# Causal attention with two MoE layers: half-empty transposed blocks put together by two, diagonal products with V in two row tiles

## The chip, the cores and the metric

One core of a Trainium2 chip runs the whole program in one launch. The metric is the device time in microseconds (us). The kernel before was run three times: 553.40, 554.47 and 555.22 us, median 554.47. One more execution was profiled.

## What is computed

Attention with a causal mask over 2 batches x 12 heads, 448 positions, 64 values per head, then two feed-forward layers, all in float32:

```
scores = (q @ k.T) / sqrt(64); scores = where(upper triangle, -1e9, scores)
attn   = exp(scores - max); attn = attn / (sum + 1e-9)
x = attn @ v                       # 896 tokens x 768
x = relu(x @ w_in)**2 @ w_out      # 768 -> 2048 -> 768
h = x @ w_in2; y = (h - tanh(h)) @ w_out2
```

The heads are taken by pairs: 12 pairs, numbered 0 to 11, pairs 0 to 5 of the first batch. The 448 positions are seven blocks of 64, numbered 0 to 6. Block c of the queries sees the blocks 0 to c of the keys, and of block c only the lower triangle.

## The kernel before, in words

A round of the main loop (line 549, number s) works on three pairs at once: the scores of pair s, exps and scaling of pair s - 1, transposes and products with V of pair s - 2, called a. From s = 8 on (`f`) one group of 18 products of the first MoE layer (`fill`) is put between the attention's parts. The order on each engine is the order in which the code is written; nothing is rescheduled.

*Scores* (`scores`, line 264). Per query block c one matmul per head, 64 rows deep: head 0 in the upper half of the array's rows, head 1 in the lower one. Float32 matmuls run in two passes, so the trace has two records for each. The results of the seven blocks stand in four banks of PSUM (tag `s`).

*Softmax* (`maxes`, `exps`, `small`, `sums`, `recips`, `norms`). VectorE (DVE) adds the mask, copies the scores to the tile `p` in SBUF and takes the row extremum. ScalarE (ACT) makes the exps in place, DVE scales them. In `p` every block c has a region of its own; `POFF` gives its start. Blocks with an odd number of 64-column key blocks are padded to 128 columns with zeros (line 252).

*Transposes* (`transposes`, line 335). TensorE (PE) turns `p` in pieces of 128 x 128: for the key chunk kc (128 keys) and each query block c that sees any of it. That is 7 + 5 + 3 + 1 = 16 pieces per pair (`TBLK`), four to a PSUM bank; ACT copies each bank to the tile `pt` (`tcopy`, line 342: four copies of 512 columns). In the pieces with c = 2 kc one half of the keys is padding.

*Products with V* (`pv`, line 348). For kc = 0, 1, 2 a matmul 128 rows deep over all query blocks from 2 kc on (448, 320, 192 columns), and for kc = 3 one of 64 rows and 64 columns, whose V rows are the tile `vend` (partitions 0 to 63). All of it adds up in one PSUM bank (`o`). The two heads write to the two halves of the bank's partitions, side by side.

*Output of attention* (`xhi`, line 369, on ACT; `xlo`, line 373, on DVE). The result is split into a high and a low float32r part for the MoE products. `xhi(a - 1)` stands before the copies of pair a on ACT, `xlo(a - 1)` between the softmax work of later pairs on DVE; the latter frees the bank `o` for pair a.

*MoE* (`pieces`, line 381): products of 128 rows by 448 columns, three for each pair of tiles (lines 387 to 389). Its weights are decoded and split by DVE and ACT (lines 107 to 137), in doses that a budget sets per round.

Of the kernel before, what the change touches and what calls it, by code (L numbers as in the profile page):

```python
# [8 lines left out]
F32 = mybir.dt.float32  # L9
# [10 lines left out]
B, H, S, D = 2, 12, 448, 64  # L20
DM = H * D
DFF = 2048
P = 128
# [4 lines left out]
NPAIR = B * NP  # L28
NQ = S // D
# [21 lines left out]

STEPS = (((6,), (5, 0)), ((3, 2), (4, 1)))
SOFF = {6: 0, 5: 0, 0: 384, 3: 0, 2: 256, 4: 0, 1: 320}
SI = {c: i for i, c in enumerate(c for st in STEPS for cs in st for c in cs)}
TURNED = {c for st in STEPS for c in st[1]}

SUMMED = (0,)

POFF = (0, 128, 256, 512, 768, 1152, 1536)

TBLK = [(kc, c) for kc in range(4) for c in range(2 * kc, NQ)]
TBASE = {kc: TBLK.index((kc, 2 * kc)) for kc in range(4)}


@with_exitstack
def body(ctx: ExitStack, tc: tile.TileContext, qT, kT, vL, w1, w2, w3, w4, out):
    nc = tc.nc
    sb = ctx.enter_context(tc.tile_pool(name="sb", bufs=1))  # L70
    ps = ctx.enter_context(tc.tile_pool(name="ps", bufs=1, space=PSUM))

    ident = sb.tile([P, P], F32, name="ident")
    mask = sb.tile([P, S], F32, name="mask")
# [125 lines left out]
    vs = {}  # L200
# [8 lines left out]
    def load_v(b):  # L209
        t = sb.tile([P, 3, DM], F32, tag=f"v{b}", name=f"v{b}")  # L210
        nc.sync.dma_start(out=t, in_=vL[b, : 3 * P].rearrange("(t p) d -> p t d", p=P))
        if b == 0:
            vs["end"] = slot(7, [D, B, DM], F32, "vend")
            nc.sync.dma_start(out=vs["end"], in_=vL[:, 3 * P :].rearrange("b p d -> p b d"))
        vs[b] = [t[:, 0], t[:, 1], t[:, 2], vs["end"][:, b]]

    load_qk(0)
# [11 lines left out]

    nc.gpsimd.memset(mask, 0.0)  # L230
    for j in range(2):
        r = mask[D * j : D * j + D, S - D :]
# [15 lines left out]
    prob = [slot(i, [P, 2048], F32, f"p{i}") for i in range(3)]  # L248
    for i in range(3):
        for c in range(0, NQ, 2):  # L250
            e = POFF[c] + D * (c + 1)
            nc.vector.memset(prob[i][:, e : e + D], 0.0)

    sc = {}
    stat = {}
    pt = {}
    tb = {}
    ob = {}
# [5 lines left out]
    def scores(n, t):  # L264
        q, k = qk[n]
        banks = []
        for z, cs in enumerate(step(n, t)):

            tag, bufs = ("s", 4) if n != 1 else ("t", 2) if t == 0 else ("oh"[z], 1)
            bank = ps.tile([P, 512], F32, tag=tag, bufs=bufs, name=f"s{n}_{t}_{z}")  # L270
            banks.append(bank)
            for c in cs:
                sc[n, c] = bank[:, SOFF[c] : SOFF[c] + D * (c + 1)]
        for i in range(2):
            for z, cs in enumerate(step(n, t)):
# [11 lines left out]
    def maxes(n, t, part=slice(None)):  # L287
        if n not in stat:
            stat[n] = sb.tile([P, 3, 8], F32, tag="stat", bufs=4, name=f"st{n}")
        st = stat[n]  # L290
        cs = blocks(n, t)[:: 1 if t or n == 0 else -1]
        for c in cs[part]:
            w = D * (c + 1)
            nc.vector.tensor_tensor_reduce(  # L294
                out=prob[n % 3][:, POFF[c] : POFF[c] + w],
                in0=sc.pop((n, c)),
                in1=mask[:, S - w :],
                scale=-0.125,
                scalar=3e38,
                op0=ALU.add,  # L300
                op1=ALU.min,
                accum_out=st[:, 0, SI[c] : SI[c] + 1],
            )
# [31 lines left out]
    def transposes(n, t):  # L335
        tag, bufs = ("h", 1) if t == 2 and n < NP else ("t", 2)
        bank = tb[n, t] = ps.tile([P, 512], F32, tag=tag, bufs=bufs, name=f"t{n}_{t}")
        for i, (kc, c) in enumerate(TBLK[4 * t : 4 * t + 4]):
            o = bank.rearrange("p (i j q) -> p i j q", j=2, q=D)[:, i, :: -1 if c in TURNED else 1]
            nc.tensor.transpose(o, prob[n % 3][:, POFF[c] + P * kc : POFF[c] + P * kc + P], ident)  # L340

    def tcopy(n, t):
        if t == 0:
            pt[n] = slot(3 + n % 2, [P, 16, P], F32, f"pt{n}")
        bank = tb.pop((n, t))
        nc.scalar.copy(out=pt[n][:, 4 * t : 4 * t + 4], in_=bank.rearrange("p (i q) -> p i q", q=P))  # L346

    def pv(n, kcs):
        b, hp = divmod(n, NP)
        if 0 in kcs:  # L350
            ob[n] = ps.tile([P, 512], F32, tag="o", bufs=1, name=f"o{n}")
        o = ob[n]
        for kc in kcs:
            r = P if kc < 3 else D
            m = NQ - 2 * kc
            for j in range(2):
                h = 2 * hp + j
                nc.tensor.matmul(  # L358
                    o[D * j : D * j + D, P * kc : S],
                    lhsT=vs[b][kc][:r, D * h : D * h + D],  # L360
                    rhs=pt[n][:r, TBASE[kc] : TBASE[kc] + m, D * j : D * j + D],
                    start=(kc == 0),
                    stop=(kc == 3),
                    skip_group_check=True,
                )
        if 3 in kcs:
# [182 lines left out]
    for s in range(NPAIR + 2):  # L549
        p, a = s - 1, s - 2  # L550
        ss, sp, sa = s < NPAIR, 0 <= p < NPAIR, a >= 0
        f = s - 2 >= NP
        if ss:
            budget[0] = min(budget[0], 0) + (SHARE_PAIR[f] if s > 1 else 0)
            e0, e1 = blocks(s, 0)[:: -1 if s else 1], blocks(s, 1)
        else:
            budget[0] = min(budget[0], 0) + SHARE_LAST
        if sp:
            exps(p, blocks(p, 1)[-1:])
        if ss:  # L560
# [24 lines left out]
        if ss:  # L585
            maxes(s, 0, slice(-1, None))
        if sp and s > 1:
            recips(p)
        if a >= 1:
            xlo(a - 1)  # L590
        if f and ss:
            one()
        if ss:
            exps(s, e0[:2])
        if s == 1:
            small(p)
            sums(p)
            recips(p)
        if sp:
            norms(p, (0, 1, 2) if ss else (0, 1, 2, 3, 4, 5, 6))  # L600
        if f:
            one()
        if f:
            for t in (2, 3):
                transposes(a, t)
                tcopy(a, t)
            fill(3)
        late()
        if ss:
            exps(s, e0[2:])  # L610
        relus()
        if ss:
            maxes(s, 1)
            exps(s, e1[:-1])
        if sp and ss:
# [74 lines left out]
```

## Time and profile before

| | us |
|---|---|
| median of three runs | 554.47 |
| the profiled execution | 554.28 |
| its span, first to last instruction | 552.4 |
| busy in the span: PE, DVE, ACT | 544.5, 347.6, 330.0 |
| granted clock of PE, mean | 1.00 |

The profiled execution takes 1.9 us more than its span. PE is TensorE's matmuls, PEld its weight loads, POOL is GpSimd. A matmul's duration holds the latency from its first row in to its last result out, and matmuls follow each other before the one ahead has ended, so that the durations of a group add up to more than the time it takes. What a matmul costs is read from the distance of two starts, or from differences of durations between sizes.

### The profile page before, as it was taken

The numbers are of one execution on the slowest core, as the hardware profiler recorded it, in microseconds if no ns is written. First come the engines' busy times: TensorE is split into PE (matmuls) and PEld (weight loads), VectorE is DVE, ScalarE is ACT, GpSimd is POOL, SyncE is SP. The second block draws the span as 40 slices with busy tenths as digits, with TensorE's granted clock in tenths as the row PEclk, the third lists the DMA queues.
The fourth block names the chain that finished last, engine by engine and source line by source line (L and its number), as shares of the span: only waits on it lengthen the run. The fifth ranks groups of instructions, "written<-read, shape, count | busy, mean of one in ns | idle before, by whom it ended". The sixth has DMA issues, their size and how long they took to land.

```text
span 552.4 us, 7889 instructions
## 1 busy us (share of the span) xinstructions
PE 544.5 (99%) x3038; PEld 480.9 (87%) x3038; DVE 347.6 (63%) x742; ACT 330.0 (60%) x630; POOL 1.6 (0%) x9
## 2 busy tenths in 40 slices
PE   8999999999999999999999999999999999999997
PEld 4667777899999999999999999999999999999996
DVE  5999998364534244453554688987654588887311
ACT  6999987577424266665333388776553677865100
POOL 1000000000000000000000000000000000000000
PEclk9999999999999999999999999999999999999999
DMA  8844223353443333331324130113755301016111
GB/s 259 299 149 132 109 82 97 108 171 115 135 152 115 114 115 114 115 114 58 114 66 163 58 115 1 57 58 90 237 188 171 114 1 58 0 59 217 55 50 51
DMA packets 15525, 61.85 MB, mean 112 GB/s; under 512 B 1664, under 2 KB 6400, under 8 KB 15488
## 3 DMA queue, kind: packets, MB, share of 16 engines
q1 hardware_dynamic: 15200, 61.00, 33.2%
q8 instruction: 24, 0.39, 0.3%
q10 hardware_dynamic: 288, 0.34, 0.2%
q14 instruction: 13, 0.11, 0.1%
HBM read 58.59 MB, written 2.75 MB: 111 GB/s over the span
## 4 chain that ended last, share of the span: by engine, by line
PE 93%; ACT 6%; DVE 1%; issue 0%; DVEq 0%
PE h L387 14%; PE h L389 14%; PE h L388 14%; PE o L387 14%; PE o L388 14%; PE o L389 14%; ACT p L312 3%; PE o L358 3%; PE t L340 2%; PE s L279 2%; ACT pt L346 2%; PE warm L224 1%; ACT raw L107 0%; DVE p L294 0%; ACT x L371 0%; DVE p L333 0%
## 5 line engine op out<-in xcount | busy, mean ns | idle before, releaser
L387 PE MATMUL o<-g,w 128*128 128x448 f32 x384 | 140.4, 366 | 0.0
L388 PE MATMUL o<-g,w 128*128 128x448 f32 x384 | 140.4, 366 | 0.0
L389 PE MATMUL o<-g,w 128*128 128x448 f32 x384 | 140.2, 365 | 0.0
L387 PEld LDWEIGHTS o<-g,w 128*128 128x128 f32 x384 | 72.1, 188 | 6.1
L389 PEld LDWEIGHTS o<-g,w 128*128 128x128 f32 x384 | 72.1, 188 | 6.0
L388 PEld LDWEIGHTS o<-g,w 128*128 128x128 f32 x384 | 72.1, 188 | 5.8
L387 PE MATMUL h<-x,w 128*128 128x448 f32 x192 | 72.3, 377 | 0.0
L388 PE MATMUL h<-y,w 128*128 128x448 f32 x192 | 70.6, 368 | 0.0
L389 PE MATMUL h<-y,w 128*128 128x448 f32 x192 | 70.6, 368 | 0.0
L389 PE MATMUL h<-x,w 128*128 128x448 f32 x192 | 70.6, 368 | 0.0
L387 PE MATMUL h<-y,w 128*128 128x448 f32 x192 | 70.6, 368 | 0.0
L388 PE MATMUL h<-x,w 128*128 128x448 f32 x192 | 70.5, 367 | 0.0
L124 ACT CAST w<-raw 128x768 fp32r<-128x768 f32 x56 | 50.5, 903 | 26.9 <-DVE raw L121 26.9
L121 DVE SCALAR_TENSOR_TENSOR raw<-raw 128x768 int32<-128x768 int32 x64 | 61.1, 954 | 5.4 <-ACT raw L107 5.4
L107 ACT ACTIVATE raw<-raw 128x768 f32<-128x768 f32 x64 | 59.1, 923 | 0.0
L137 DVE TENSOR_TENSOR w<-raw,w 128x768 fp32r<-128x768 f32 x32 | 30.6, 957 | 35.0 <-ACT w L124 34.8
L400 DVE TENSOR_TENSOR g<-r,g 128x448 fp32r<-128x448 f32 x32 | 20.0, 625 | 48.0 <-ACT g L397 48.0
L527 ACT COPY part<-o 128x448 f32<-128x448 f32 x24 | 12.8, 534 | 57.0 <-PE o L389 57.0
L135 DVE SCALAR_TENSOR_TENSOR w<-w,raw 128x768 fp32r<-128x768 f32 x32 | 30.6, 956 | 23.3 <-ACT w L124 23.3
L312 ACT ACTIVATE p<-p,st 128x256 f32<-128x256 f32 (+6 forms) x84 | 40.8, 516 | 4.2 <-DVE st L294 4.2
L387 PEld LDWEIGHTS h<-x,w 128*128 128x128 f32 x192 | 36.1, 188 | 4.0 <-issue 0.7
L389 PEld LDWEIGHTS h<-y,w 128*128 128x128 f32 x192 | 36.0, 188 | 3.4
(57 smaller groups left out, 718.5 us busy)
## 6 DMA issues: line engine op xcount, KB each, us to landing
raw<-w SPq DMA_DIRECT2D x64, 768.0 KB, 4.3
q<-qT SPq DMA_DIRECT2D x12, 224.0 KB, 5.3
k<-kT SPq DMA_DIRECT2D x11, 224.0 KB, 3.8
out<-part SPq DMA_DIRECT2D x11, 224.0 KB, 1.9
v<-vL SPq DMA_DIRECT2D x2, 1152.0 KB, 7.7
vend<-vL SPq DMA_DIRECT2D x1, 384.0 KB, 11.4
k<-kT ACTq DMA_DIRECT2D x1, 224.0 KB, 3.5
out<-part ACTq DMA_DIRECT2D x1, 112.0 KB, 1.7
```

The source lines that it names most:

```text
L107: nc.scalar.activation(h, h, AF.Prelu, scale=2.0**-112, alpha=2.0**32)
L121: nc.vector.scalar_tensor_tensor(out=lo, in0=hi, scalar=3, in1=lo, op0=ALU.logical_shift_left, op1=ALU.bitwise_or)
L124: act_late.append(lambda: nc.scalar.copy(out=st["w"][:, 0], in_=lo.bitcast(F32)))
L135: nc.vector.scalar_tensor_tensor(out=w[:, 1], in0=w[:, 0].bitcast(F32), scalar=-(1.0 - 2.0**-24), in1=f, op0=ALU.mult, op1=ALU.add)
L137: nc.vector.tensor_sub(out=w[:, 1], in0=f, in1=w[:, 0])
L312: nc.scalar.activation(p, p, AF.Exp, bias=st[:, 0, i : i + 1], scale=-1.0, **kw)
L358: nc.tensor.matmul(o[D * j : D * j + D, P * kc : S], lhsT=vs[b][kc][:r, D * h : D * h + D], rhs=pt[n][:r, TBASE[kc] : TBASE[kc] + m, D * j ...
L387: nc.tensor.matmul(h, lhsT=hi, rhs=xh, start=(k == 0), stop=False)
L388: nc.tensor.matmul(h, lhsT=hi, rhs=xl, start=False, stop=False)
L389: nc.tensor.matmul(h, lhsT=lo, rhs=xh, start=False, stop=(k == kk - 1))
L400: nc.vector.tensor_sub(out=dst[1], in0=v, in1=dst[0])
L527: nc.scalar.copy(out=part[m][:, b], in_=o)
```

## The change

The keys are stored in the order 6, 0, 1, 2, 3, 5, 4 (`KEYS`), and the regions of `p` are packed so that the diagonal block of 0 stands beside that of 6, and that of 2 beside that of 4. Each of these two pairs is turned by one transpose of 128 columns: one diagonal block then stands on partitions 0 to 63, the other on 64 to 127. The other 12 pieces have 128 full keys. So there are 14 pieces in place of 16, and the fourth copy has 256 columns.

The full products with V have 384, 256 and 128 columns. The diagonal blocks 0 and 2 (first half of `ENDS`, z = 0) and 6 and 4 (second half, z = 1) are products of 64 rows and 64 columns, the first half in the upper half of the array's rows, the second in the lower one, adding into the same bank. Between the two halves stands a wait: a memset of POOL on a tile `token` waits for the first half's last product, and the second half's first product waits for that memset. `vend` moves to partitions 64 to 127. The score matmul of block 4 is cut in two (64 and 256 columns), since its keys don't stand together any more. The mask is wider (704 columns), because the diagonal block is no longer always the last. The memsets of padding are gone.

In the loop the second half of pair a - 1 stands behind the scores of pair s; in the last two rounds, without scores, it stands behind the products of the pair after. The output parts of pairs 9 and 10 come later, and the banks of pairs 10 and 11 are of tag `s`.

```diff
+KPART = {c: ((0, D, D * (c + 1)),) for c in range(6)}
+KPART[4] = ((0, 6 * D, D), (D, D, 4 * D))
+KPART[6] = ((0, 0, S),)
-POFF = (0, 128, 256, 512, 768, 1152, 1536)
-TBLK = [(kc, c) for kc in range(4) for c in range(2 * kc, NQ)]
+KEYS = (6, 0, 1, 2, 3, 5, 4)
+POFF = (0, 1024, 512, 1152, 704, 1408, 64)
+DIAG = (0, 1, 2, 3, 0, 4, 0)
+TBLK = [(kc, (c,)) for kc in range(3) for c in range(2 * kc + 1, NQ)]
+ENDS = ((0, 6), (2, 4))
+TBLK += [(None, cs) for cs in ENDS]
...
-                        nc.tensor.matmul(sc[n, c][e : e + D], lhsT=q[r, D * c : D * c + D], rhs=k[r, : D * (c + 1)], start=(c == cs[0]), stop=(c == cs[-1]), skip_group_check=True)
+                        for o, a, w in KPART[c]:
+                            nc.tensor.matmul(sc[n, c][e : e + D, o : o + w], lhsT=q[r, D * c : D * c + D], rhs=k[r, a : a + w], start=(c == cs[0] and o == 0), stop=(c == cs[-1]), skip_group_check=True)
...
+        e = min(4 * t + 4, NT)
+        nc.scalar.copy(out=pt[n][:, 4 * t : e], in_=bank.rearrange("p (i q) -> p i q", q=P)[:, : e - 4 * t])
...
+    def pv(n):
+        tag, bufs = ("o", 1) if n < NPAIR - 2 else ("s", 4)
+        ob[n] = ps.tile([P, 512], F32, tag=tag, bufs=bufs, name=f"o{n}")
+        for kc, i in enumerate(TBASE):
+            m = NQ - 2 * kc - 1
             for j in range(2):
+                product(n, j, slice(S - D * m, S), kc, slice(0, P), pt[n][:, i : i + m, D * j : D * j + D], start=(kc == 0), stop=False)
+        pv_ends(n, 0)
+    def pv_ends(n, z):
+        for i, cs in enumerate(ENDS):
+            c = cs[z]
+            for j in range(2):
+                r, e = slice(D * z, D * z + D), D * (j ^ (c in TURNED))
+                ins = product(n, j, slice(D * c, D * c + D), c // 2, r, pt[n][r, NT - 2 + i, e : e + D], start=False, stop=(z == 1 and i == 1))
+                if z == 1 and i == j == 0:
+                    tc.add_manual_dep(ins, passed.pop(n), WAITS, reason="row tiles of one bank")
+        if z == 0:
+            p = nc.gpsimd.memset(token, 0.0).ins
+            tc.add_manual_dep(p, ins.name, WAITS, reason="row tiles of one bank")
+            passed[n] = p.name
...
             scores(s, 0)
             scores(s, 1)
+            if a >= 1:
+                pv_ends(a - 1, 1)
...
-        if a >= 1:
+        if a >= 1 and ss:
             xhi(a - 1)
+        if a == NPAIR - 1:
+            xhi(a - 2)
...
         if sa:
-            pv(a, range(4))
+            pv(a)
+            if not ss:
+                pv_ends(a - 1, 1)
...
+    pv_ends(NPAIR - 1, 1)
+    xhi(NPAIR - 2)
+    xlo(NPAIR - 2)
     xhi(NPAIR - 1)
     xlo(NPAIR - 1)
```

Between pair 1's products and pair 2's transposes PE's order was this (o1, pt1: bank and transposed tile of pair 1; s4: scores of pair 4; x2 at the end: both heads; 128x2x64: a piece whose heads are swapped):

```order
L358 MATMUL o1_375<-pt1_332,v0_108 64x192 [waits Activation_49]
L358 MATMUL o1_375<-pt1_332,v0_108 64x192
L358 MATMUL o1_375<-pt1_332,vend_110 64x64 x2
L279 MATMUL s4_0_0_387<-k4_185,q4_184 64x448 [waits DMAHW4_49,DMAHW3_49]
...
L279 MATMUL s4_1_1_396<-k4_185,q4_184 64x128 x2
L340 MATMUL t2_0_413<-ident_63,p2_116 128x2x64 [waits PE_49]
```

With the change it is this:

```order
L369 MATMUL o1_375<-pt1_334,v0_108 64x128 x2
L369 MATMUL o1_375<-pt1_334,v0_108 64x64 [waits Activation_49]
L369 MATMUL o1_375<-pt1_334,v0_108 64x64 x3
L289 MATMUL s4_0_0_390<-k4_178,q4_177 64x448 [waits DMAHW4_49,DMAHW3_49]
...
L289 MATMUL s4_1_1_399<-k4_178,q4_177 64x128 x2
L369 MATMUL o1_375<-pt1_334,vend_110 64x64 [waits Pool_49]
L369 MATMUL o1_375<-pt1_334,vend_110 64x64
L369 MATMUL o1_375<-pt1_334,v0_108 64x64 x2
L357 MATMUL t2_0_422<-ident_63,p2_116 128x2x64 [waits PE_49]
```

Two small products of the first half follow at once, and behind the scores, before the next transposes, stand the four of the second half with the wait on POOL.

At the end of the attention part, where no scores are left, PE's order is now this (h6: the first product of the MoE layer behind it):

```order
L369 MATMUL o11_1381<-pt11_1337,v1_481 64x64 [waits Activation_49]
L369 MATMUL o11_1381<-pt11_1337,v1_481 64x64 x3
L369 MATMUL o10_1308<-pt10_1255,vend_110 64x64 [waits Pool_49]
L369 MATMUL o10_1308<-pt10_1255,vend_110 64x64
L369 MATMUL o10_1308<-pt10_1255,v1_481 64x64 x2
L369 MATMUL o11_1381<-pt11_1337,vend_110 64x64 [waits Pool_49]
L369 MATMUL o11_1381<-pt11_1337,vend_110 64x64
L369 MATMUL o11_1381<-pt11_1337,v1_481 64x64 x2
L417 MATMUL h6_0_1412<-x0_66,w6_1306 128x448 [waits DVE_49]
```

Before, two products of 64 rows stood here between the 128-row ones and h6. Now pair 11's second half stands right behind its first half and pair 10's second half.

## Rows read from the trace of the kernel before

**Rows 1.** The page: busy us of the engines, share of the span, instructions.
```profile
PE 544.5 (99%) x3038; PEld 480.9 (87%) x3038; DVE 347.6 (63%) x742; ACT 330.0 (60%) x630; POOL 1.6 (0%) x9
```

**Rows 2.** Windows: stretch, length; busy us of PE, PEld, DVE, ACT, POOL; PE's clock; DMA.
```profile
38.20:49.10 10.90, 9.91 (x110) 6.76 (x109) 10.90 (x47) 10.90 (x35) 0.00 (x0) 1.00 0.43 154
58.30:67.50 9.20, 9.20 (x81) 7.20 (x79) 8.86 (x32) 8.16 (x24) 0.00 (x0) 1.00 0.26 88
```

**Rows 3.** Chain that ended last, merged: start us, us on the chain, engine and line.
```profile
28.27 3.34 ACT p L312 x13
59.16 0.87 PE t L340 x8
```

**Rows 4.** Timeline of DVE: start us, us, instruction, idle time before and its releaser.
```profile
20.26 0.17 DVE L322 TENSOR_SCALAR st<-st 128x7 f32<-128x7 f32 x1 [0.39 <-ACT p L312]
38.15 0.17 DVE L322 TENSOR_SCALAR st<-st 128x7 f32<-128x7 f32 x1 [0.86 <-ACT p L312]
67.19 0.62 DVE L400 TENSOR_TENSOR g<-r,g 128x448 fp32r<-128x448 f32 x1 [0.30 <-ACT g L397]
```

**Rows 5.** Groups by line and shape, whole span: count, busy us, mean ns of one.
```profile
L312 ACT ACTIVATE p<-p,st 128x448 f32<-128x448 f32 x12 | 8.2, 684 | 0.0
L312 ACT ACTIVATE p<-p,st 128x64 f32<-128x64 f32 x12 | 4.3, 369 | 0.0
L358 PE MATMUL o<-pt,v 128*64 128x320 f32 x48 | 8.6, 432 | 0.0
L358 PE MATMUL o<-pt,v 128*64 128x192 f32 x48 | 6.0, 326 | 0.0
```

**Rows 6.** Timeline of PE around pair 6's products with V: start us, us, instructions.
```profile
54.22 0.36 PE L388 MATMUL h<-x,w 128*128 128x448 f32 x1
54.42 0.37 PE L389 MATMUL h<-x,w 128*128 128x448 f32 x1
54.72 1.84 PE L358 MATMUL o<-pt,v 128*64 128x448 f32 x12
56.49 0.27 PE L358 MATMUL o<-pt,vend 64*64 64x64 f32 x2
...
58.27 0.47 PE L387 MATMUL h<-x,w 128*128 128x448 f32 x1
```

**Rows 7.** Timeline of PE, pair 5: the 64-row product with V and the scores after.
```profile
47.30 0.27 PE L358 MATMUL o<-pt,vend 64*64 64x64 f32 x2
47.32 0.59 PE L279 MATMUL s<-k,q 64*64 64x448 f32 x2
47.41 0.23 PE L358 MATMUL o<-pt,vend 64*64 64x64 f32 x2
47.46 0.54 PE L279 MATMUL s<-k,q 64*64 64x448 f32 x2
```

**Rows 8.** Timelines and POOL's groups: what one engine's end releases on another.
```profile
86.61 0.51 ACT L371 CAST x<-o 128x448 fp32r<-128x448 f32 x1
87.02 0.58 ACT L346 COPY pt<-t 128x512 f32<-128x512 f32 x1
87.65 0.33 PE L340 MATMUL t<-ident,p 128*128 128x128 f32 x1 [0.34 <-ACT pt L346]
100.01 0.33 PE L358 MATMUL o<-pt,vend 64*64 64x64 f32 x4
100.27 0.47 PE L387 MATMUL h<-x,w 128*128 128x448 f32 x1
L230 POOL MEMSET mask<- 128x448 f32 x1 | 0.5, 471 | 0.3 <-POOLq L683 0.3
L683 POOL MEMSET const-bfloat16-1.0<- 128x1 bf16 x1 | 0.1, 102 | 0.0
```

**Rows 9.** Timelines of PE and ACT, pair 3: the first four transposes and their copy.
```profile
31.34 0.49 PE L340 MATMUL t<-ident,p 128*128 128x128 f32 x3
31.92 0.58 ACT L346 COPY pt<-t 128x512 f32<-128x512 f32 x1
```

More of the change, by code (lines that the diff above doesn't have):

```diff
@@ L59 @@
 SUMMED = (0,)
-POFF = (0, 128, 256, 512, 768, 1152, 1536)
-TBLK = [(kc, c) for kc in range(4) for c in range(2 * kc, NQ)]
-TBASE = {kc: TBLK.index((kc, 2 * kc)) for kc in range(4)}
+KEYS = (6, 0, 1, 2, 3, 5, 4)
+POFF = (0, 1024, 512, 1152, 704, 1408, 64)
+DIAG = (0, 1, 2, 3, 0, 4, 0)
+BEFORE = D * max(DIAG)
+TBLK = [(kc, (c,)) for kc in range(3) for c in range(2 * kc + 1, NQ)]
+TBASE = [TBLK.index((kc, (2 * kc + 1,))) for kc in range(3)]
+ENDS = ((0, 6), (2, 4))
+FRONT = {c for _, c in ENDS}
+TBLK += [(None, cs) for cs in ENDS]
+NT = len(TBLK)
 @with_exitstack
@@ L73, in body @@
     ident = sb.tile([P, P], F32, name="ident")
-    mask = sb.tile([P, S], F32, name="mask")
+    mask = sb.tile([P, BEFORE + S], F32, name="mask")
     abias = sb.tile([P, 1], F32, name="abias")
@@ L212, in load_v @@
         if b == 0:
-            vs["end"] = slot(7, [D, B, DM], F32, "vend")
-            nc.sync.dma_start(out=vs["end"], in_=vL[:, 3 * P :].rearrange("b p d -> p b d"))
+            vs["end"] = slot(7, [P, B, DM], F32, "vend")
+            nc.sync.dma_start(out=vs["end"][D:], in_=vL[:, 3 * P :].rearrange("b p d -> p b d"))
         vs[b] = [t[:, 0], t[:, 1], t[:, 2], vs["end"][:, b]]
@@ L231, in body @@
     for j in range(2):
-        r = mask[D * j : D * j + D, S - D :]
+        r = mask[D * j : D * j + D, BEFORE : BEFORE + D]
         nc.gpsimd.affine_select(out=r, in_=r, compare_op=ALU.is_ge, fill=-8e9, base=0, pattern=[[-1, D]], channel_multiplier=1)
@@ L246, in hbank @@
         return ps.tile([P, 512], F32, tag=tag, bufs=bufs, name=name)[:, :S]
[L248 to L252, printed above, removed]
+    prob = [slot(i, [P, NQ * (NQ + 1) // 2 * D], F32, f"p{i}") for i in range(3)]
     sc = {}
@@ L296, in maxes @@
                 in0=sc.pop((n, c)),
-                in1=mask[:, S - w :],
+                in1=mask[:, BEFORE - D * DIAG[c] :][:, :w],
                 scale=-0.125,
@@ L337, in transposes @@
         bank = tb[n, t] = ps.tile([P, 512], F32, tag=tag, bufs=bufs, name=f"t{n}_{t}")
-        for i, (kc, c) in enumerate(TBLK[4 * t : 4 * t + 4]):
-            o = bank.rearrange("p (i j q) -> p i j q", j=2, q=D)[:, i, :: -1 if c in TURNED else 1]
-            nc.tensor.transpose(o, prob[n % 3][:, POFF[c] + P * kc : POFF[c] + P * kc + P], ident)
+        for i, (kc, cs) in enumerate(TBLK[4 * t : 4 * t + 4]):
+            o = bank.rearrange("p (i j q) -> p i j q", j=2, q=D)[:, i]
+            c = cs[0]
+            if kc is None:
+                src = prob[n % 3][:, POFF[c] + D * c :][:, :P]
+            else:
+                g = POFF[c] + P * kc + (D if c in FRONT else 0)
+                src = prob[n % 3][:, g : g + P]
+                o = o[:, :: -1 if c in TURNED else 1]
+            nc.tensor.transpose(o, src, ident)
@@ L342, in tcopy, with product @@
     def tcopy(n, t):
         if t == 0:
-            pt[n] = slot(3 + n % 2, [P, 16, P], F32, f"pt{n}")
+            pt[n] = slot(3 + n % 2, [P, NT, P], F32, f"pt{n}")
         bank = tb.pop((n, t))
-        nc.scalar.copy(out=pt[n][:, 4 * t : 4 * t + 4], in_=bank.rearrange("p (i q) -> p i q", q=P))
-    def pv(n, kcs):
+        e = min(4 * t + 4, NT)
+        nc.scalar.copy(out=pt[n][:, 4 * t : e], in_=bank.rearrange("p (i q) -> p i q", q=P)[:, : e - 4 * t])
+    def product(n, j, o, kc, rows, rhs, **flags):
@@ L349, in pv @@
         b, hp = divmod(n, NP)
[L350 to L355, printed above, removed]
-            for j in range(2):
[L357 to L365, printed above, removed]
@@ L366, in pv @@
-        if 3 in kcs:
+        h = 2 * hp + j
+        return nc.tensor.matmul(ob[n][D * j : D * j + D, o], lhsT=vs[b][kc][rows, D * h : D * h + D], rhs=rhs, skip_group_check=True, **flags).ins
+    def pv(n):
[3 more added lines that the diff above has]
+            m = NQ - 2 * kc - 1
+            for j in range(2):
+                product(n, j, slice(S - D * m, S), kc, slice(0, P), pt[n][:, i : i + m, D * j : D * j + D], start=(kc == 0), stop=False)
+        pv_ends(n, 0)
@@ new lines, in body @@
+    passed = {}
+    token = sb.tile([P, 1], F32, name="token")
+    def pv_ends(n, z):
[10 more added lines that the diff above has]
+            passed[n] = p.name
+        if z == 1:
@@ L588, in body @@
             recips(p)
-        if a >= 1:
+        if a >= 1 and ss:
             xlo(a - 1)
+        if a == NPAIR - 1:
+            xlo(a - 2)
         if f and ss:
@@ L672, in pairs, with values @@
         return np.ascontiguousarray(t.reshape(B, NP, 2, S, D).transpose(0, 1, 2, 4, 3)).reshape(B, NP, P, S)
+    def values(t):
+        t = np.ascontiguousarray(t.transpose(0, 2, 1, 3)).reshape(B, NQ, D, DM)
+        return np.ascontiguousarray(t[:, [0, 1, 2, 3, 5, 4, 6]]).reshape(B, S, DM)
     arrays = {
         "qT": pairs(inputs["q"]),
-        "kT": pairs(inputs["k"]),
-        "vL": np.ascontiguousarray(inputs["v"].transpose(0, 2, 1, 3)).reshape(B, S, DM),
+        "kT": pairs(np.concatenate([inputs["k"][:, :, D * c : D * c + D] for c in KEYS], 2)),
+        "vL": values(inputs["v"]),
         "w1": w_in(inputs["moe_w_in"]),
```

1 line of the change is left out of this document (added).

## The prediction

> **What bounds the kernel now.** I read the page first, then a table of windows, then the chain of waits, then single stretches. The page shows TensorE (PE) busy 544.5 us, 99% of the span [rows 1], but busy is not the same as bound, so the table decides. From 38.2 to 49.1 us VectorE (DVE) and ScalarE (ACT) are full and PE is not (9.91 of 10.90); from 58.3 to 67.5 PE is full and DVE has a little left (8.86 of 9.20) [rows 2]. The granted clock is 1.00 in both, the 2.4 GHz level, and nothing here idles PE long enough to expect another. So the attention part has two stretches: up to about 48 us the pairs of heads are paced by ACT and DVE, from there on by PE. After 100.3 us come only products of the two MoE layers, in which the change touches nothing; whatever is won before is kept.
>
> The chain shows the same: at 28 us 13 exps of ACT in a row, at 59 us eight transposes of PE [rows 3]. In the first stretch DVE idles only twice, 0.39 and 0.86 us, both times for ACT [rows 4]. It has 1.25 us to give, so no saving on PE or ACT can win more there.
>
> **The change part by part.** *Transposes.* 14 instead of 16 per pair. Eight take 0.87 us on the chain [rows 3], 0.109 each: **-0.22 us of PE per pair**. The fourth copy out of PSUM has 256 columns instead of 512. ACT's exps fall from 684 ns at 448 columns to 369 at 64 [rows 5], 0.82 ns per column, so it saves 0.21 us per pair on ACT.
>
> *Full products with V.* 384, 256 and 128 columns instead of 448, 320 and 192: 64 fewer in each of three, in two passes each, the two heads side by side. Matmul times include a latency, so only differences count: 432 - 326 ns for 128 columns [rows 5], 0.83 ns per column. 3 x 2 x 64 x 0.83 = **-0.32 us per pair**.
>
> *Diagonal products.* Before: one block of 64 rows, two passes, in the upper row tile. Now: two blocks there (four passes), and behind the scores two more in the lower row tile (four passes). Both kinds of array shape occur before in the same order, and each change of shape costs about 0.09 us (two h matmuls stand 0.20 apart, from h to V 0.30 [rows 6]); their number stays. What happens in the 64-row shape is seen at 47.30: the V product starts in the upper tile, 0.02 us later head 1's scores start in the lower one, its second pass comes at 47.41, and head 0's scores start at 47.46 [rows 7]. So the row tiles run side by side. In pair 6 the stretch from that product to MoE is 1.78 us (56.49 to 58.27 [rows 6]), 1.69 less the change of shape, set by the upper tile. There two passes are added: 0.11. The lower tile starts 0.14 earlier but shows two weight loads of some 0.05 uncovered, so I estimate its end 0.06 earlier, at 1.63; four passes of 0.055 and the split of score block 4 (64 + 256 columns, no more columns, 0.02) give 1.87. The later one counts: **+0.17 us per pair**. Bounds for an added pass: 0.05 (47.41 to 47.46) and 0.11 (47.30 to 47.41) [rows 7]. I take the lower, because the higher stands where the shape has just changed and no weights could be loaded ahead. That makes +0.11 to +0.5 per pair.
>
> Here the Trainium skill speaks against the change: its page "TensorEngine Tiling (Array Packing)", section "Instruction Overhead", gives every matmul about 60 cycles of overhead and advises against tiling by a size that is already small. By that, an estimate from the page, 0.025 us would go on top of each of six small passes a pair, and the sum would come out at 552.4. The 0.05 us for a pass of 64 columns shows no such addition [rows 7].
>
> *The new wait.* The first product of the second half waits for a POOL memset that waits for the first half. It stands in PE's queue, and behind it all of PE: the transposes, ACT's copies, the next pair. No row shows PE-POOL-PE. Lower bound: the last pass's own time 0.22 (two of them 0.23 [rows 7]), 0.09 from PE to another engine (the fourth transpose ends at 31.34 + 0.49 = 31.83, ACT starts at 31.92 [rows 9]), 0.10 for a 128x1 memset, 0.05 back (ACT's copy ends at 87.60, PE starts at 87.65 [rows 8]): 0.46 us. Upper bound: POOL's longest row, 0.47, with the longest idle time of its group before it, 0.30, in place of 0.10: 1.13 us [rows 8]. I take 0.46, as the work is the 128x1 row's. The cover is head 1's scores: from the start of the first half's last pass (0.11 + 2 x 0.055 = 0.22 after its first) to 1.63, so 1.41 us. Cost 0 in pairs 0 to 8; behind pairs 9 and 10 the next pair's transposes and products come between. Without scores behind it stands **pair 11** only: 0.22 + 0.46 + four passes (0.27) + 0.09 = 1.04 instead of 0.26 (from 100.01 to 100.27 [rows 8]), **+0.79**, up to 1.45.
>
> *xhi and o.* The output bank is complete about 1.9 us later, behind the scores, so ACT's cast waits there now with copies and exps behind it. It costs nothing as long as the transposes come still later: at 31.92 ACT's copy follows the fourth transpose by those 0.09, so it waits for PE already, and the cast (0.41 before its copy) has its data about then. DVE's subtraction (xlo) frees the bank for the next V, in DVE's order as before. Pair 9's cast and subtraction move a round later: the cast out of the way of the copies at 87.02 (86.61 to 87.02 is 0.41 [rows 8]); the subtraction takes the place that pair 10's had. The twelve memsets gone from DVE's start and the wider mask on POOL lie before the first scores are read; cost 0.
>
> **The sum**, against the profiled execution's own 554.28 us (0.2 under the median of the three, 554.47):
> - First stretch: ACT saves 0.21 in each of the pairs 0 to 3 before DVE's idle time at 38.15, 0.84 in all. But its copies wait for PE too, whose margin at 31.9 is 0.09 + 0.15 that PE itself gains between V and the transposes (0.32 - 0.17), on top of 0.21 from the first idle time [rows 4]; so about 0.45, and 0.21 of the last copy: **-0.7** (bounds 0 and -1.25).
> - Pair 5, from V to the scores' end, first under PE: -0.32 + 0.17 = **-0.15**.
> - Pairs 6, 7, 8: 3 x (-0.22 - 0.32 + 0.17) = **-1.1**.
> - Pairs 9 and 10, no scores behind V, both tiles side by side: 2 x (-0.22 - 0.32 + 0.11) = **-0.86**.
> - The stop of PE before 87.65 (0.34 of idle time [rows 8]) ends 0.41 earlier, while PE comes 0.21 earlier from pair 9: **-0.2**.
> - Pair 11: -0.22 - 0.32 + 0.79 = **+0.25**.
>
> Together -2.8 us: **551.5 us**. All bounds at their good end give 550.7, all at their bad one 554.6.
>
> **The rivals.**
> (a) *DVE keeps the pace.* It is full from 38.2 to 49.1 [rows 2] and idles 0.30 at 67.19 [rows 4], less than the 0.37 of a pair. Then the first stretch wins nothing, pair 5 neither, and a pair in the second 0.30: -2.8 + 0.7 + 0.15 + 0.2, 552.5 us. Against it: both idle times of the first stretch are for ACT.
> (b) *Small passes cost double*, 0.11 each as after a change of shape. Six passes at 0.055 above my price: +0.33 in pairs 5 to 8, four (+0.2) in pairs 9 to 11: -2.8 + 1.9, 553.4 us. For it: the pass at 47.30; against it: the one at 47.41. By the page named above, of the Trainium skill, it would be half of that.
> (c) *POOL answers late: slower.* If PE-POOL-PE takes R, each of the pairs 0 to 8 loses R - 1.41, and pair 11 R - 0.46. 10 R = 2.8 + 9 x 1.41 + 0.46 gives the point from which the change loses: R = 1.6 us. At 2.0 us it is 9 x 0.59 + 1.54 - 2.8 = +4.1, 558.4 us. Against it: the rows allow 1.13 at most; for it: POOL has no work after the first microseconds, so nothing shows how it wakes.
> That the change does not do what it says is excluded by the order: 14 transposes, and the wait on Pool, stand there.
>
> **How the numbers follow.** About 0.3%, 1.7 us, is what a measurement of this kernel can tell from no change. My forecast (550.5 to 552.7) 0.52, (a) 0.18, (b) 0.18, (c) 0.08, the rest 0.04. Faster by over 1.7 us, so under 552.8: nearly all of the forecast, some 0.6 of (a), a little of (b): 0.62. Same: the rest of those: 0.28. Slower: (c) and strays: 0.10. The range takes in the forecast, (a) and most of (b), with the spread of the runs before below: 550.2 to 554.0.
>
> **What would show it.** Steps right: V's first 64-row product comes 1.45 us after V's start instead of 1.77 (54.72 to 56.49), and MoE 1.95 after that instead of 1.78 (to 58.27 [rows 6]); DVE's idle time at 38 us is nearly gone; before 100 us PE stops once for POOL, about 0.5 us. Wrong: PE idle before the second half's products in every pair (c), 64-column passes 0.11 apart throughout (b), the first stretch's pairs at 5.5 to 5.7 us as before with DVE free of idle time (a).

## The result and the profile after

The changed kernel takes **548.40 us** (median of four, 548.29 to 548.79) against 554.17 for the kernel before in the same series: a ratio of 0.9898, with a 95% interval of 0.9883 to 0.9912. That is 5.8 us less, where 2.8 were forecast; the range began at 550.2, so the time lies below it. The sign was right, the size was not.

The page of the changed kernel: its busy line (it answers to [rows 1]), the granted clock and a group of MoE products:

```profile
span 546.6 us, 8248 instructions
PE 538.0 (98%) x3206; PEld 483.6 (88%) x3206; DVE 345.8 (63%) x730; ACT 327.9 (60%) x630; POOL 4.2 (1%) x21
PEclk9999999999999999999999999999999999999999
...
L417 PE MATMUL h<-y,w 128*128 128x448 f32 x192 | 69.7, 363 | 0.0
```

PE's timeline of the changed kernel (start us, us, engine, line, operation, count, idle time before and its releaser), where attention ends and at the last MoE product:

```profile
98.37 0.33 PE L369 MATMUL o<-pt,vend 64*64 64x64 f32 x4 [0.26 <-POOL token L393]
98.53 0.28 PE L369 MATMUL o<-pt,v 64*64 64x64 f32 x4
98.75 0.48 PE L417 MATMUL h<-x,w 128*128 128x448 f32 x1
...
542.89 0.37 PE L419 MATMUL o<-g,w 128*128 128x448 f32 x1
```

The same timeline of the kernel before, its last product:

```profile
548.71 0.36 PE L389 MATMUL o<-g,w 128*128 128x448 f32 x1
```

Attention ends at 98.75 instead of 100.27 [rows 8]: 1.52 us earlier. From there to the last product it is 444.14 us instead of 448.44: **4.30 us come from the two MoE layers, whose instructions are the same in both kernels.** Each layer runs in two halves, and each half has two stages: products into h, then products into o. Here is layer one's second half, first in the kernel before, then in the changed one: the first and the last product of its h stage, and of its o stage.

```profile
195.89 0.36 PE L387 MATMUL h<-x,w 128*128 128x448 f32 x1
...
254.82 0.37 PE L389 MATMUL h<-x,w 128*128 128x448 f32 x1
255.02 0.36 PE L387 MATMUL o<-g,w 128*128 128x448 f32 x1
...
313.37 0.36 PE L389 MATMUL o<-g,w 128*128 128x448 f32 x1
```

```profile
193.75 0.36 PE L417 MATMUL h<-x,w 128*128 128x448 f32 x1
...
251.16 0.36 PE L419 MATMUL h<-x,w 128*128 128x448 f32 x1
251.37 0.36 PE L417 MATMUL o<-g,w 128*128 128x448 f32 x1
...
310.00 0.37 PE L419 MATMUL o<-g,w 128*128 128x448 f32 x1
```

A stage has 288 products, so 287 distances. The h stage falls from 58.93 to 57.41 us, 205.3 to 200.0 ns a product; the o stage rises from 58.35 to 58.63, 203.3 to 204.3 ns. PE is not idle in either and the granted clock is the same. What did change for these products is where their operands stand in a partition of SBUF: the wider mask, the smaller tiles `p` and `pt` and the 4-byte token (32 after rounding) push the tiles behind them. The operands are these: the weights are in the ring of tiles w, the moving operand (the one that streams through the array) of an h product is a tile x (y in the second layer, in the same place), that of an o product one of eight tiles, the g slots. The traces hold no addresses; those in this text follow from the order and the sizes in which a kernel creates its tiles.

### The profile page after: what moved, and what is told of

It reads as the page before. It is cut to its first block, busy times and chain, and to the rows that moved or that the text cites. A ratio compares the mean times of both kernels' runs of the same rounds, so it can differ in the third digit from the quotient of the medians.

```text
span 546.6 us, 8248 instructions
## 1 busy us (share of the span) xinstructions
PE 538.0 (98%) x3206; PEld 483.6 (88%) x3206; DVE 345.8 (63%) x730; ACT 327.9 (60%) x630; POOL 4.2 (1%) x21
## 4 chain that ended last, share of the span: by engine, by line
PE 92%; ACT 4%; DVE 3%; issue 0%; DVEq 0%; POOLq 0%; ACTq 0%
PE o L419 14%; PE o L418 14%; PE o L417 14%; PE h L417 14%; PE h L419 14%; PE h L418 14%; PE o L369 3%; ACT p L322 2%; PE t L357 2%; PE s L289 2%; DVE p L304 1%; DVE p L343 1%; ACT pt L364 1%; PE warm L238 1%; ACT raw L121 0%; DVE x L405 0%
## 5 line engine op out<-in xcount | busy, mean ns | idle before, releaser
L417 PE MATMUL h<-x,w 128*128 128x448 f32 x192 | 71.5, 372 | 0.0
L417 PE MATMUL h<-y,w 128*128 128x448 f32 x192 | 69.7, 363 | 0.0
L419 PE MATMUL h<-y,w 128*128 128x448 f32 x192 | 69.6, 362 | 0.0
L419 PE MATMUL h<-x,w 128*128 128x448 f32 x192 | 69.5, 362 | 0.0
L418 PE MATMUL h<-x,w 128*128 128x448 f32 x192 | 69.4, 362 | 0.0
L418 PE MATMUL h<-y,w 128*128 128x448 f32 x192 | 69.1, 360 | 0.0
```

What stands on the lines that cost most here:

```text
L417: nc.tensor.matmul(h, lhsT=hi, rhs=xh, start=(k == 0), stop=False)
L418: nc.tensor.matmul(h, lhsT=hi, rhs=xl, start=False, stop=False)
L419: nc.tensor.matmul(h, lhsT=lo, rhs=xh, start=False, stop=(k == kk - 1))
```

## The experiments: what moved the MoE layers

Three theories: A, the place of the weights against the moving operand; B, the sizes of the big tiles; C, not addresses but the other stream of instructions. The first four runs change addresses alone.

**e1: the kernel before with a tile that nothing uses.**

```diff
+    pad = sb.tile([P, 1], F32, name="pad")
+    nc.gpsimd.memset(pad, 0.0)
     sc = {}
```

> The kernel before, with one tile more: 4 bytes in every partition, which the allocator rounds up to 32, created where the change creates its token, and cleared once by POOL. Everything created after it, the ring of weights w and four of the eight g slots among it, stands 32 bytes further (w at 32 instead of 0 modulo 64 bytes); no instruction of PE, ACT or DVE changes. Theory A (the place of the weights in SBUF against the moving operand sets the pace of the MoE products): the four stages of h products take 57.4 us instead of 58.9 each, the four of o products 0.3 more, as in the changed kernel: 549.4 us instead of 554.2, and down to 548.5 if the h products in the attention part gain as well. Theory B (it was the 1,024 bytes by which mask, probability and transposed tiles moved the others) and theory C (not addresses, but the other stream of instructions): 554.2 us, h stages 58.9.

549.56 us, ratio 0.992 (0.9906 to 0.9935). Thirty-two bytes give 4.5 us. PE's timeline, the same h stage and the end of attention:

```profile
99.97 0.47 PE L389 MATMUL h<-x,w 128*128 128x448 f32 x1
...
194.93 0.36 PE L389 MATMUL h<-x,w 128*128 128x448 f32 x1
...
252.34 0.36 PE L391 MATMUL h<-x,w 128*128 128x448 f32 x1
```

57.41 us, as in the changed kernel, from the token's 32 bytes alone and without a new stream of PE's instructions. Theory A stands; B and C fall.

**e2, e3, e4: the changed kernel with a token of 64 bytes; with everything from x on 32 bytes further; with both.**

```diff
-    token = sb.tile([P, 1], F32, name="token")
+    token = sb.tile([P, 16], F32, name="token")
...
-    abias = sb.tile([P, 1], F32, name="abias")
+    abias = sb.tile([P, 9], F32, name="abias")[:, :1]
```

> The changed kernel with a token tile of 64 bytes instead of 4 (32 after rounding): what is created after it stands 32 bytes further, w at 0 modulo 64 again. Theory A: the h stages are back at 58.9 us, o stages at 58.35, so the MoE layers lose 4.8 us: 553.2 us, and up to 554.0 if h products in the attention part lose too. Theories B and C: 548.4 us as in the changed kernel.

> The changed kernel with everything from the x tiles on 32 bytes further: x at 0 instead of 32 modulo 64 and w at 0 instead of 32, so that their distance is that of the changed kernel. If the distance between moving operand and weights counts (A1), h stages stay at 57.4 us and the time at 548.4. If the place of the weights alone counts (A2), h stages are back at 58.9: about 553.2 us. Theories B and C: 548.4.

> The changed kernel with x 32 bytes further (0 modulo 64) and everything behind the token 64 bytes further (w at 32 modulo 64 as in the changed kernel; all eight g slots at 32 as well). If the distance between x and w counts (A1), h stages are slow at 58.9 us, and o stages, where g and w now agree, fast at about 57.4: 548.4 + 6.0 - 5.0, about 549 us. If the place of the weights alone counts (A2): 548.4 us, h stages 57.4, o stages 58.6. Theories B and C: 548.4 us.

552.23 us (0.997, 0.9958 to 0.9981), 547.77 (0.9894, 0.9877 to 0.991) and 551.05 (0.9949, 0.9934 to 0.9964). e2 loses 3.8 of the 5.8 us again. e3, with both places moved and their distance kept, loses nothing: the distance counts, not the place (A1). e4's h stages are slow as A1 says; its total lies 2 us above the 549 worked out, as h is slower than in the kernel before (206.6 ns) and o less fast than hoped (202.0).

**e5, e6: all agreeing modulo 64 bytes,** the changed kernel and the kernel before.

```diff
-    nc.scalar.activation(sb.tile([P, 1], F32, name="warmexp"), abias, AF.Exp)
+    nc.scalar.activation(sb.tile([P, 9], F32, name="warmexp")[:, :1], abias, AF.Exp)
```

(e5 has e2's token as well.)

> The changed kernel with two small tiles rounded up to 64 bytes instead of 32 (warmexp and the token), so that x, all eight g slots and the w ring stand at 32 modulo 64 bytes; no instruction changes. If the distance between moving operand and weights modulo 64 bytes counts, h stages stay at 57.4 us and o stages fall from 58.6 to 58.0 as in the two runs whose g slots all agreed with w: 548.4 - 4 x 0.65 = 545.8 us. If agreement in one place costs as much in another: 548.4 or more.

> The kernel before with one small tile (warmexp) rounded up to 64 bytes instead of 32, so that x, g and w all stand at 32 modulo 64; no instruction changes. By the distance: h stages 57.4 instead of 58.9, o stages 58.0 to 58.35, attention 0.3 less: 554.0 - 4 x 1.5 - (0 to 1.4) - 0.3 = 546.3 to 547.7 us, which is less than the changed kernel as handed over. Against it the run above then gives what the change itself is worth when addresses are equal: by the attention stretch of the earlier runs -1.2 to -1.3 us; by the forecast -2.8.

548.47 us (0.9898, 0.9883 to 0.9913) and 548.71 (0.9907, 0.9891 to 0.9922): both misses. In e5 o gained (201.9 ns), but h went to 202.7; in e6 h came to 200.0, but o stayed at 203.5. Modulo 64 was too coarse. Sorted by the weights' address less the moving operand's modulo 128 the stages fell into four classes, and e9 to e11 were set up for the fastest one, 64.

**e9, e10, e11: difference 64 modulo 128** in the changed kernel, the kernel before, and e8 (below), by wider small tiles and unused pads ahead of the w ring and of two g slots.

```diff
+        if u == 0:
+            sb.tile([P, 16], F32, name="pad0")
...
+            if (l, half, m, b) == (0, 0, 0, 0):
+                sb.tile([P, 16], F32, name="pad1")
```

> The changed kernel, no instruction changed, with x and all eight g slots at 32 modulo 128 bytes and the w ring at 96, by wider small tiles and two pads of 64 bytes. The rule read from the runs so far: the spacing of two MoE products follows the weights' address less the moving operand's, modulo 128 bytes: 200.0 ns at 64, about 202.7 at 0, 205.3 at 32, 206.6 at 96. By it h stages and o stages all take 57.4 us: 548.4 - 4 x 1.2 = 543.6 us. If the rule holds for h alone and something else sets the o stages: 545.8 to 548.4 us.

> The kernel before, no instruction changed, with its addresses arranged as in the run above. By the rule all eight stages take 57.4 us: 554.0 - 4 x 1.5 - 4 x 0.95 - 0.3 = 543.9 to 544.8 us, the upper end from 549.6 (w moved by 32 bytes alone) less 4 x 1.2. The run above should then be faster than this one by what the change's instructions are worth, 1.2 us by the attention stretch; by the forecast's steps it would be 2.8.

> The changed kernel with the second half of the diagonal products between the two steps of scores and with the addresses of the first run of this group. The two gains add: 547.8 - 4.8 = 543.0 us, about 0.6 below the first run of this group. If the gain of the middle place came from elsewhere, as much as the first run.

545.13 us (0.9835, 0.9821 to 0.9848), 548.22 (0.9888, 0.9874 to 0.9901), 544.95 (0.983, 0.9816 to 0.9843): faster, yet 1.5 to 4 us short of the rule. e10's h stages took 202.2 ns at the same 64 modulo 128 at which e1's took 200.0. Modulo 256 the two differ, 64 and 192. With that every stage of every run so far stands in one table (distance of two products in ns, from the first and last start of a stage in the traces; where g slots fall into two classes both are given):

```
kernel             h: diff  ns      o: diff of the g slots       ns
before             160      205.3   128 (4 slots), 0 (4)         203.3
after, e1, e3      192      200.0   160 (4), 0 (4)               204.3
e2, e4             224      206.6   192 (4), 0 (4)               202.0
e5                 0        202.7   192 (4), 0 (4)               201.9
e6                 192      200.0   128 (4), 0 (4)               203.5
e9, e11            192      200.0   64 (6), 192 (2)              201.9
e10                64       202.2   192 (6), 64 (2)              201.1
e14, e15, e16      192      200.0   192 (8)                      200.0
```

Within the changed kernel's o stages the products of the slots at 160 stand 205.3 to 205.9 ns apart, those at 0 201.6 to 204.2. So in a mixed stage the slots at one difference don't all have one pace. Two stages don't fit: the shorter first h stage took 204.4 in e2 and 200.0 in e4, where later ones took 206.6. What else plays a part there stays open. Differences of 32 and 96 were not run. The wider mask and the smaller `p` and `pt` move others by multiples of 1,024 bytes, which is nothing modulo 256: of the change's moves only the token's 32 bytes count in this table, as e1 shows.

**e14, e15, e16: every difference at 192 modulo 256,** with the pads of e9 resized (0.6 KB a partition in all; e15 has one pad more).

> The changed kernel, no instruction changed, with every g slot and x at 160 modulo 256 bytes and the weights at 96, so that the weights' address less the moving operand's is 192 modulo 256 everywhere. Rule D256, from the runs so far (spacing of two products by that difference: 200.0 ns at 192, 202.2 at 64, 202.7 at 0, about 203.4 at 128, 205.3 to 205.9 at 160, 206.6 at 224): all eight stages take 57.4 us, 545.1 - 4 x 0.53 = 543.0 us. If o stages have a pace of their own: 545.1, as with six of the eight slots at 64.

> The kernel before, no instruction changed, with every difference at 192 modulo 256 bytes. D256: all stages at 57.4 us; 548.2 - 4 x 0.64 (h, 58.05 to 57.4) - 4 x 0.32 (o, 57.73 to 57.4) - 0.15 in the attention part = 544.2 us, so that the changed kernel at 192 is 1.2 us faster than this one. If the change is worth 2.8 at equal pace, as forecast: 545.8.

> The changed kernel with the second half of the diagonal products between the two steps of scores, every difference at 192 modulo 256. D256: 544.95 - 4 x 0.53 = 542.8 us, the fastest of all.

**543.03 us** (0.9797, 0.9784 to 0.9811), **544.54** (0.9825, 0.9811 to 0.9838) and **542.63** (0.979, 0.9777 to 0.9803): all three within 0.4 of what was written down. e14's timeline, an h stage and the o stage behind it, 57.40 us each:

```profile
98.59 0.47 PE L419 MATMUL h<-x,w 128*128 128x448 f32 x1
...
192.31 0.36 PE L419 MATMUL h<-x,w 128*128 128x448 f32 x1
...
249.71 0.36 PE L421 MATMUL h<-x,w 128*128 128x448 f32 x1
249.91 0.36 PE L419 MATMUL o<-g,w 128*128 128x448 f32 x1
...
307.31 0.36 PE L421 MATMUL o<-g,w 128*128 128x448 f32 x1
```

So at equal pace the change's own instructions are worth 544.54 - 543.03 = 1.5 us, about half of the forecast (e1 and the changed kernel, whose differences agree too, give 549.56 - 548.40 = 1.2), and the kernel before with pads beats the changed kernel as handed over by 3.9 us. By its median e16 is the fastest kernel of the study.

## The experiments: the attention part

e1 is the fair partner here: its differences are those of the changed kernel, in h and in o. Pair 7's round in e1, then in the changed kernel:

```profile
63.88 0.60 PE L360 MATMUL o<-pt,v 128*64 128x448 f32 x2
...
65.64 0.27 PE L360 MATMUL o<-pt,vend 64*64 64x64 f32 x2
65.66 0.59 PE L281 MATMUL s<-k,q 64*64 64x448 f32 x2
65.75 0.23 PE L360 MATMUL o<-pt,vend 64*64 64x64 f32 x2
65.81 0.54 PE L281 MATMUL s<-k,q 64*64 64x448 f32 x2
...
67.43 0.48 PE L389 MATMUL h<-x,w 128*128 128x448 f32 x1
...
73.00 0.59 PE L360 MATMUL o<-pt,v 128*64 128x448 f32 x1
```

```profile
63.36 0.54 PE L369 MATMUL o<-pt,v 128*64 128x384 f32 x2
...
64.80 0.38 PE L369 MATMUL o<-pt,v 64*64 64x64 f32 x5
64.97 0.59 PE L289 MATMUL s<-k,q 64*64 64x448 f32 x1
...
65.03 0.23 PE L369 MATMUL o<-pt,v 64*64 64x64 f32 x2
65.08 0.54 PE L289 MATMUL s<-k,q 64*64 64x448 f32 x2
...
66.68 0.27 PE L369 MATMUL o<-pt,v 64*64 64x64 f32 x1
66.73 0.22 PE L369 MATMUL o<-pt,vend 64*64 64x64 f32 x1
66.79 0.28 PE L369 MATMUL o<-pt,v 64*64 64x64 f32 x3
67.00 0.48 PE L417 MATMUL h<-x,w 128*128 128x448 f32 x1
...
72.36 0.54 PE L369 MATMUL o<-pt,v 128*64 128x384 f32 x2
```

From MoE to the next V 5.36 instead of 5.57 us: two transposes less, -0.21 as forecast. From V to the first 64-row product 1.44 instead of 1.76: -0.32 as forecast. From there to MoE 2.20 instead of 1.79: **+0.41, forecast +0.17**. So a round gains 0.12 instead of 0.37. The added passes hold up the scores of *both* row tiles. In the lower tile, whose scores start while the first half still fills the upper one, the first scores come 0.17 behind the first 64-row product (64.97) instead of 0.02 (65.66). In the upper tile they come 0.28 behind it (65.08) instead of 0.17 (65.81), behind the first half's last passes.

**e7: without the split of score block 4.**

```diff
-KPART[4] = ((0, 6 * D, D), (D, D, 4 * D))
+KPART[4] = ((0, D, 5 * D),)
```

> The changed kernel without the split of score block 4: its scores come from one product of 320 columns instead of 64 and 256 (keys 0 to 3 and 5 in place of 0 to 4, so the scores of one block are other ones). If the split is what makes the scores end 0.18 us later than before (measured from the first product of 64 rows), that stretch from 64-row product to MoE falls from 2.19 to 2.0 us in pairs 5 to 8: 547.7 us. If it is the first half's added passes that hold up the scores of both row tiles, the stretch falls by 0.06 at most: 548.2 us.

547.54 us (0.9881, 0.9864 to 0.9897). Pair 7:

```profile
62.96 0.54 PE L369 MATMUL o<-pt,v 128*64 128x384 f32 x2
...
66.48 0.48 PE L417 MATMUL h<-x,w 128*128 128x448 f32 x1
```

3.52 us from V to MoE instead of 3.64: the split costs 0.12 a pair, not 0.02. From V of pair 5 to V of pair 9 it is 35.54 us (45.19 to 80.73) instead of 36.02, the same 0.12 in each of four pairs. That is half of the excess of 0.24; the expectation had put all of it or 0.06 on it.

**e8: the second half between the two steps of scores** (`pv_ends(a - 1, 1)` moved up one line).

> The changed kernel with the second half of the diagonal products behind the first step of the next pair's scores instead of behind both, in pairs 0 to 9. Theory L (in the first stretch the output bank is complete too late: PE stops 0.44 us twice before V for DVE's subtraction, ACT waits 0.1 to 0.2 for the bank): these stops are gone and the first MoE product at 49 us comes 0.3 to 0.5 earlier, 548.0 us. Theory D (DVE's own work paces that stretch, the stops of PE are only what is left over): the time is 548.4, with the same 0.7 us of idle time of DVE at 38 us. If POOL's answer is needed before it is there (it is ready some 0.5 to 0.7 us after the last pass of the first half, and the first step of scores covers about 0.85), PE stops before the second half in pairs 5 to 8 and the time is 549 us or more.

547.84 us (0.9886, 0.9871 to 0.9901). The total is that of theory L, the place is not: from V of pair 1 to V of pair 5 it takes 23.73 us (20.88 to 44.61, with a stop of PE as before, now for ScalarE's copy), as in the changed kernel, 23.69 (21.66 to 45.35). A gain shows in the second stretch, 53.02 us from V of pair 5 to MoE (44.61 to 97.63) instead of 53.40, where the small passes now run between score passes. V of pair 0 comes earlier as well, at 14.54 instead of 15.30, but that is no work of this edit: in e3, with the changed kernel's instructions, it comes at 14.69. POOL's answer is there in time all the same.

```profile
44.61 0.55 PE L369 MATMUL o<-pt,v 128*64 128x384 f32 x2 [0.51 <-ACT pt L364]
```

**e12 and e13: less of DVE, less of ScalarE in the first stretch.**

```diff
+            if c == 6 and n < 5:
+                continue
```

```diff
-            w = D * (c + 1)
+            w = D if c == 6 and n < 6 else D * (c + 1)
```

> The changed kernel without VectorE's scaling of the largest score block (448 columns, 0.44 us) in pairs 0 to 4, so five operations of DVE less before V of pair 5. Theory D (DVE's own work paces the first stretch): V of pair 5 comes up to 2.2 us earlier, at 43.2 to 44.5 instead of 45.35, and the time falls by as much. Theory S (ScalarE's exps and copies pace it, DVE only waits in other places): V of pair 5 comes less than 0.5 us earlier and DVE's idle time grows by the rest.

> The changed kernel with ScalarE's exp of the largest score block cut to its first 64 columns in pairs 0 to 5 (the other columns stay without exp): 0.3 us less of ScalarE in each, six before V of pair 5. Theory S (ScalarE paces the first stretch): V of pair 5 comes 1.2 to 1.8 us earlier against V of pair 0, 28.3 to 28.9 us behind it instead of 30.05. Theory R (no engine alone: ScalarE, DVE and PE wait for each other in a ring, as taking 0.12 a pair from PE won 0.13 in all and 0.44 a pair from DVE 0.4): about 0.4 us earlier, and the idle time shows up on ScalarE.

547.73 and 547.53 us, one run each. The timelines at V of pairs 0 and 5, e12 and e13, and behind them from 14 to 50 us DVE's waits in e12 and ScalarE's in e13 (us in total, times, longest):

```profile
15.10 0.54 PE L371 MATMUL o<-pt,v 128*64 128x384 f32 x2
...
44.75 0.54 PE L371 MATMUL o<-pt,v 128*64 128x384 f32 x2 [0.45 <-DVE x L407]
...
DVE st L332 <- ACT p L322: 2.1, 3, 1.1
```

```profile
14.64 0.54 PE L369 MATMUL o<-pt,v 128*64 128x384 f32 x2
...
44.61 0.54 PE L369 MATMUL o<-pt,v 128*64 128x384 f32 x2 [0.45 <-DVE x L405]
...
ACT pt L364 <- PE t L357: 1.0, 2, 0.8
ACT x L401 <- PE o L369: 0.7, 1, 0.7
```

From V of pair 0 to V of pair 5 it takes 29.65 and 29.97 us, against 30.05 in the changed kernel (15.30 to 45.35). Runs with the changed kernel's instructions differ there: 29.88 in e14, 30.20 in e9. So of the four scalings left out on the way (1.8 us) some 0.4 came back (0.2 to 0.55 by the run that it is set against), and of the four shortened exps (1.2 us) nothing that is clear of this spread. Counted from V of pair 1 e13 seems to gain more, 23.00 against 23.69; but there V of pair 1 had come later, 6.97 us behind V of pair 0 instead of 6.36, and e9, with V of pair 1 late in the same way (6.87), shows 23.33 with nothing left out. Neither D nor S holds. With less of DVE, DVE's waits for ScalarE grow from 1.0 to 2.1 us; with less of ScalarE, ScalarE's waits for PE grow from 0.2 to 1.7. That fits theory R, the ring, but it is one run each, and what share each engine has stays open.

## Why the prediction was wrong

**The step that failed:** "After 100.3 us come only products of the two MoE layers, in which the change touches nothing; whatever is won before is kept." The instructions are untouched; their operands' addresses are not, and with them went 4.3 of the 5.8 us. The MoE products inside the attention part gained as well: it ends at 99.97 in e1 instead of 100.27. The forecast had this term at nothing. The profile of before shows the pace of 205.3 ns but not that it could be another one; the diff shows that tiles move, and I did not follow them through the allocation. The other step that failed is the price of the diagonal products beside scores (below): the change's own instructions won 1.2 to 1.5 us, not 2.8. The two errors have opposite signs: at the forecast's price for the instructions the time would lie lower still.

The attention part by the sum's own steps, the changed kernel against e1 (starts of V, us; the last row ends at MoE; V of pair 0 starts at 15.29 in e1 and 15.30 in the other):

```
                          e1              after           gain   forecast
up to V of pair 5         45.62           45.35           -0.27  -0.7
V(5) to V(6)              45.62 to 54.75  45.35 to 54.35  -0.13  -0.37
V(6) to V(9)              54.75 to 82.13  54.35 to 81.37  -0.36  -1.11
V(9) to V(11)             82.13 to 97.94  81.37 to 96.19  -0.99  -1.06
V(11) to MoE              97.94 to 99.97  96.19 to 98.75  +0.53  +0.47
```

- *Transposes, full products with V, pairs 9 and 10, pair 11*: right. PE stops for POOL once, 0.26 us in the row at 98.37, and in pair 7 the memset starts 0.35 us behind the first half's last passes (65.03 to 65.38):

```profile
65.38 0.23 POOL L393 MEMSET token<- 128x1 f32 x1 [8.83 <-PE o L369]
```

  Behind scores PE never waits for it. Rival (c) is out.
- *Diagonal products beside scores*: mis-sized, +0.41 a round instead of +0.17 (rows above). The failing sentence is that the lower row tile's end comes 0.06 earlier. It counts on that tile's scores starting 0.02 behind the first 64-row product, as before; they start 0.17 behind it, so the tile begins 0.15 later. And splitting a score block costs 0.12 (e7), not 0.02. With these two sizes the prediction's own sum for the lower tile is 1.63 + 0.15 + 4 x 0.055 + 0.12 = 2.12 us, 2.21 with the change of shape; 2.20 were measured. That PE hands out its products in the order of the program, so that a pass that waits for its tile holds up those for the other, would explain the 0.15; no run tests it. In pairs 5 to 8 all this took 1 us of the forecast, though not beyond the bound of +0.5.
- *Rival (b)*, every small pass 0.11 apart, is out: at 66.68, 66.73 and 66.79 they start 0.05 to 0.06 apart. The overhead of about 60 cycles that the Trainium skill, "TensorEngine Tiling (Array Packing)", section "Instruction Overhead", gives every matmul is not seen there as an addition to each pass; that section's own example, that a matmul of one column takes as long as one of 60, makes it a least time rather, which 64 columns can't show. The small tiles cost more than forecast all the same, by the two sizes above.
- *First stretch*: -0.27, less than the -0.7 of the sum and nearer to rival (a), whose sign, DVE without idle time, is not there. "It costs nothing as long as the transposes come still later", said of the late output bank, leaves out a wait. Waits of PE and DVE from 14 to 50 us in the changed kernel, then DVE's in e1 (us in total, times, longest):

```profile
PE t L357 <- ACT pt L364: 1.3, 2, 0.7
PE o L369 <- DVE x L405: 0.9, 2, 0.4
...
DVE st L332 <- ACT p L322: 1.0, 2, 0.7
```

```profile
DVE st L324 <- ACT p L314: 1.2, 2, 0.9
```

  PE stops twice for DVE's subtraction to free the bank, which it doesn't in e1, and DVE's idle time falls by 0.2 of 1.25 only [rows 4]. By e8 this wait is not the cause of the small gain: there PE stops for ScalarE instead, and V of pair 5 comes no earlier behind V of pair 0 (30.07 us, 14.54 to 44.61, against 30.05). What keeps the gain small stays open; e12 and e13 fit engines that wait for each other in turn.

## What to carry to other kernels

Before a change is credited with its time, compare a stage that it does not touch; if that stage moved, look at the addresses. A change that resizes or adds an SBUF tile moves every tile behind it, so measure it against the old kernel with a pad that gives the old operands the new places; here 32 bytes counted, and moves by 1,024 did not. In a kernel of back-to-back products, choose the places of weights and moving operands on purpose: here 0.6 KB of padding a partition won 9.6 us in the kernel before and 5.4 in the changed one, where the change's instructions won 1.5.

## What the runs showed of the hardware

Back-to-back products of 128x128 weights with 448 columns in four bytes started 200.0 to 206.6 ns apart at the granted clock of 1.00 (the 2.4 GHz level), by the weights' address less the moving operand's modulo 256 bytes: 200.0 at 192, 202.2 at 64, 202.7 at 0, 205.3 at 160, 206.6 at 224; between 203 and 204 where half the slots stood at 128. Two places moved together by 32 bytes changed nothing (e3). These are the paces of whole stages with one difference; one short stage at 224 took 200.0 (e4), so the difference is not the whole rule.

An obvious rival is that other engines' accesses get in the way. The kernel before answers it: in these two h stages (length; busy us of PE, PEld, DVE, ACT, POOL; PE's clock; DMA) DVE is busy for 28.82 and 51.52 us and DMA for 0.35 and 0.17 of the time, and the products stand 205.3 ns apart in both.

```profile
196.00:254.70 58.70, 58.70 (x288) 53.66 (x287) 28.82 (x40) 40.50 (x64) 0.00 (x0) 1.00 0.35 119
313.60:372.40 58.80, 58.80 (x288) 53.77 (x287) 51.52 (x87) 46.80 (x83) 0.00 (x0) 1.00 0.17 54
```

That the loading of weights, which runs beside the product ahead of it, gets in the way of that product's reading would fit; nothing here shows it. The Trainium skill, "SBUF — State Buffer", section "SBUF: two separate sides", says of the engine side that only GpSimd's and VectorE's shared ports cause contention and that PE never waits on anyone. In these runs each product takes 6.6 ns, 3%, longer at 224 than at 192, with every instruction the same; whether that is PE's own two reads in each other's way, which that sentence would not allow, the runs can't tell.
